# Two transformer layers: second chunk's token load, MLP weight loads and a norm buffer moved in the ramp, with a new instruction order

## The chip, the cores and the metric

The kernel runs on one core of a Trainium2 chip. The metric is the device time of one execution in microseconds (us), lower is better. Five engines work side by side: TensorE (PE) multiplies, VectorE (DVE), ScalarE (ACT) and GpSimd (POOL) compute on tiles, and SyncE (SP) issues the transfers (DMAs), transposing ones among them. Each engine runs its instructions strictly in the order in which the program holds them, and waits on semaphores for the others.

## The reference

The input is 2048 tokens of 576 features. Two layers of the same form run one after the other, with the same weights in both:

```python
qkv = (x @ wqkv) ... # 32 heads of 18 features
scores = einsum("bhqd,bhkd->bhqk", q, k) * (Dh ** -0.5)
mask = (idx[:, None] - idx[None, :] >= 0) & (idx[:, None] - idx[None, :] < 256)
p = softmax(where(mask, scores, -1e9))
o = einsum("bhqk,bhkd->bhqd", p, v)
A_ref = o ... @ wo
h = gelu(einsum("bsd,df->bsf", layernorm(x), w1) + b1)   # 576 -> 4608
B_ref = einsum("bsf,fd->bsd", h, w2) + b2                # 4608 -> 576
x = x + A_ref(layernorm(x));  x = x + B_ref(layernorm(x))   # twice
```

## The kernel before

**Tiles and chunks.** The tokens are cut into 16 tiles of 128, four tiles to a chunk, so that each layer has four chunks and the program eight (`k` from 0 to 7). A chunk goes through these steps: layer norm of its four tiles (`ln1_in` for the input tokens), with each normalised tile transposed into a buffer; projections to queries, keys and values (`qkv`); attention (`E0` for the first chunk, `E` for the others) in eight groups of four heads with up to three score pieces and one value product each; the output projection with residual, second norm and its transpose (`tail`); and the MLP, in three parts of a first matmul with gelu (`G_part`) and a second matmul (`mm2`). The attention of one chunk is interleaved with the MLP of the chunk before. Neither the ramp (first chunk's norm, projections, attention) nor the end has a partner of that kind.

**Buffers.** `xnTa` holds the transposed norm that the projections read, `xnTm[:, 0]` and `xnTm[:, 1]` the transposed norm that the MLP reads, for even and odd chunks. `x_in` is the upper half of the residual tensor `x_res`, seen as bf16; the input tokens are loaded there. `w1_sb` has three slots for blocks of the first MLP matrix, each filled by one large transfer and two small ones (`w1_load`). In traces the names are those of the tensors: a load of tokens shows as `x_res<-in_A_x_dram`, one of either MLP matrix as `w_sb<-in_B_w_dram`.

**Order.** Nothing is written out by hand. Every operation is handed to a planner (`Plan.add`) with the names that it reads and writes, an estimated cost and latency, and a priority. The planner then walks through time (`schedule`): of all operations whose predecessors are done it takes the one that can start earliest on its engine, and among equal starts the one with the lower priority number. The result is a fixed order on every engine; semaphore waits follow from the names. A table `PL.nudge` adds an offset of up to 300 in either direction to the priority of every named stage (`q0.v2` is the value projection of the first chunk's third tile, `ea3.1` a score group, `ld0` the loads of the ramp, and so on), which outweighs the priorities in the code. Where the planner foresees an idle PE in the first 140 us, it puts in matmuls on a zero tile (`warm_fn`, line 674) that compute nothing.

**The ramp's loads.** SP first issues the tokens of the first four tiles and the three weight matrices for queries, keys and values. What follows hangs on gates, names of results that a load reads only so as to be issued behind them:

- the tokens of tiles 4 to 7 (second chunk) read `xa3`, the last transposed norm tile of the first chunk;
- the tokens of tiles 8 to 11 (third chunk) and both bias loads read `k3`, the first chunk's last transposed key tile;
- of the first three blocks of the MLP's first matrix, the first reads `v0h0` (a value cast), the second reads `qx0`, a name that nothing has written at that point, so that it has no gate at all, and the third reads `aq2` (an attention group).

The norm of the first chunk is transposed on PE, as are its key tiles; the norm tiles of the second and third chunk and the query tiles are transposed by DMAs that SP issues (line 741 for norms, line 880 for queries and keys).

Lines that the prediction names: 626 is every plain transfer, 687 and 691 the norm's statistics, 700 and 702 its reciprocal root on POOL, 797 the projections of the first chunk, 778 and 781 those of the second chunk and all of the MLP's second matmul (one wide matmul, or four narrow ones side by side), 837 the projections of later chunks, 909 the scores, 919 the exponential, 940 the mask, 957 the value product, 1093 the MLP's first matmul.

Of the kernel before, what the change touches and what calls it, by code (L numbers as in the profile page):

```python
# [435 lines left out]
def build_kernel(nc, A_x, A_wqkv, A_wo, B_x, B_w1, B_b1, B_w2, B_b2, out):  # L436
    D = 576
# [41 lines left out]
    PL.nudge = {"": -86.31, "b": 23.63, "ea0.0": -264.23, "ea0.1": 170.66, "ea0.2": 170.75, "ea0.p0": -91.12, "ea0.p1": 0.1, "ea0.p2":  # L479
# [187 lines left out]
    for i in OUT:  # L667
        b = Bank((i,))
        add("pe", lambda e, b=b: zero(e, b), reads=["warm"], writes=[b], cost=0.25, lat=0.2, prio=-7, alloc=[b])
# [665 lines left out]
```

## Time and profile before

| | us |
|---|---|
| median of 3 runs | 863.51 |
| lowest, highest | 863.23, 866.3 |
| the profiled execution | 864.07 |
| its span in the trace | 862.3 |

| engine | busy us | share of the span |
|---|---|---|
| PE, matmuls | 846.4 | 98% |
| PE, weight loads | 520.0 | 60% |
| ACT | 601.2 | 70% |
| DVE | 395.7 | 46% |
| POOL | 378.6 | 44% |

The span runs from the first instruction to the last; the 1.8 us between it and the execution's own time lie around it. Matmuls are pipelined, so a busy PE is not a PE at its peak. In the views, "L741" is line 741 of the kernel; a row of the timeline gives start, duration, engine, line, operation, what it writes and reads, how many instructions were merged and, in brackets, the idle time before them with what ended it. "SPq" is the queue from which SP issues transfers. A granted clock of 1.00 is TensorE's full speed.

### The profile page before, as it was taken

The page shows a single profiled execution, that of the slowest core. Times are in us where ns is not written, and L with a number is a line of the kernel's source. Part 1 is how long each engine was busy: PE and PEld are TensorE (multiplying, and loading weights), DVE is VectorE, ACT ScalarE, POOL GpSimd, SP SyncE. Part 2 cuts the span into 40 slices and gives each one's busy share as a digit, 9 for nine tenths or more (in the row PEclk, how much of TensorE's full clock was granted, in tenths as well). Part 3 has the DMA queues.
Part 4 walks back from the last instruction along what each step waited for, and adds up shares of the span by engine and source line. Part 5 has one row for each costly group of instructions (what it writes and reads, how often), then busy time and mean ns, then how long its engine had stood idle before and what let it go on. Part 6 is the DMA issues. An engine that isn't in the chain of part 4 may idle for free.

```text
span 862.3 us, 27890 instructions
## 1 busy us (share of the span) xinstructions
PE 846.4 (98%) x12002; PEld 520.0 (60%) x12002; DVE 395.7 (46%) x949; ACT 601.2 (70%) x757; POOL 378.6 (44%) x563
## 2 busy tenths in 40 slices
PE   8899999999999999999999999999999999999998
PEld 6455556556565565666665655656556555556556
DVE  5787334644356442673426723465223633153012
ACT  5798797688757797476774878738777589853730
POOL 3787454375234662254522655416444276331100
PEclk9999999999999999999999999999999999999999
DMA  9798534743577524985359353594434963446320
GB/s 235 143 187 142 140 96 136 165 126 66 167 161 150 140 72 138 176 142 170 102 124 192 85 164 124 99 204 108 154 122 104 250 190 105 135 133 179 120 84 29
DMA packets 181995, 119.84 MB, mean 139 GB/s; under 512 B 107504, under 2 KB 181872, under 8 KB 181872
## 3 DMA queue, kind: packets, MB, share of 16 engines
q1 hardware_dynamic: 181872, 118.05, 55.6%
q8 instruction: 95, 1.56, 0.8%
q14 instruction: 28, 0.23, 0.1%
HBM read 90.10 MB, written 2.36 MB: 107 GB/s over the span
## 4 chain that ended last, share of the span: by engine, by line
PE 88%; DMA 4%; DVE 2%; POOL 2%; ACT 2%; issue 1%; SPq 0%; POOLq 0%; ACTq 0%
PE ps L1093 30%; PE ps L778 25%; PE ps L781 10%; PE ps L837 8%; PE ps L909 6%; PE ps L957 4%; PE ps L1048 3%; DMA xnTm<-xn 2%; ACT pT L919 1%; DMA xnTa<-xn 1%; PE ps L797 1%; POOL pT L940 1%; DVE xn L718 1%; DVE x_res L1025 1%; DMA qT<-qn 1%
## 5 line engine op out<-in xcount | busy, mean ns | idle before, releaser
L940 POOL TENSOR_SCALAR_AFFINE_SELECT pT<-pT 128x512 bf16<-128x512 bf16 (+1 forms) x368 | 284.3, 794 | 234.7 <-ACT pT L919 228.9
L919 ACT ACTIVATE pT<-ps 128x1024 bf16<-128x1024 f32 (+1 forms) x384 | 345.5, 972 | 49.9 <-PE ps L909 49.2
L1093 PE MATMUL ps<-xnTm,w_sb 64*128 64x512 bf16 x2592 | 290.9, 376 | 1.1 <-DVE vA L849 0.7
L1103 ACT ACTIVATE hT<-ps,b1col 128x512 bf16<-128x512 f32 x276 | 168.1, 688 | 175.3 <-PE ps L1093 175.0
L1093 PEld LDWEIGHTS ps<-xnTm,w_sb 64*128 64x128 bf16 x2592 | 129.6, 94 | 140.4 <-issue 4.8
L778 PE MATMUL ps<-w_sb,hT 128*128 128x288 bf16 x1446 | 193.7, 287 | 1.5 <-DVE x_res L1025 0.7
L1025 DVE TENSOR_TENSOR x_res<-ps,x_res 128x288 f32<-128x288 f32 x224 | 100.3, 453 | 183.5 <-PE ps L778 128.9
L778 PEld LDWEIGHTS ps<-w_sb,hT 128*128 128x128 bf16 x1446 | 133.6, 98 | 52.6 <-issue 17.1
L837 PE MATMUL ps<-wqkv,xnTa 64*128 64x288 bf16 x1296 | 90.8, 283 | 1.8 <-DMA xnTa<-xn 0.6
L781 PE MATMUL ps<-w_sb,hT 128*32 128x288 bf16 x2664 | 91.6, 286 | 0.2
L861 DVE CAST qn<-ps 128x288 bf16<-128x288 f32 x112 | 45.7, 448 | 99.1 <-PE ps L837 88.9
L837 PEld LDWEIGHTS ps<-wqkv,xnTa 64*128 64x128 bf16 x1296 | 61.6, 94 | 28.8 <-issue 3.1
L781 PEld LDWEIGHTS ps<-w_sb,hT 128*32 128x32 bf16 x2664 | 68.4, 97 | 14.9 <-issue 4.6
L968 DVE STREAM_TRANSPOSE oq<-ps 128x512 f32<-128x512 f32 x64 | 45.7, 714 | 66.6 <-PE ps L957 65.5
L909 PE MATMUL ps<-qT,kT 32*128 32x384 bf16 (+2 forms) x1216 | 64.2, 277 | 2.8 <-ACT pT L919 1.6
L700 POOL TENSOR_SCALAR vtmp<-mv_all 128x1 f32<-128x1 f32 (+1 forms) x43 | 8.9, 207 | 111.8 <-DVE mv_all L691 108.3
L687 DVE BATCH_NORM_STATS2 st_all<-x_res 128x6 f32<-128x288 f32 (+1 forms) x128 | 53.5, 445 | 9.0 <-DMA x_res<-in_A_x_dram 8.2
L1109 POOL TENSOR_TENSOR x_res<-x_res,b2bc 128x576 f32<-128x576 f32 x32 | 40.2, 1277 | 39.1 <-ACT hT L1103 38.9
L849 DVE CAST vA<-ps 128x288 bf16<-128x288 f32 x60 | 25.0, 447 | 56.6 <-PE ps L837 55.6
L957 PE MATMUL ps<-pT,vA 128*20 128x384 bf16 (+2 forms) x1408 | 50.4, 275 | 0.0
L909 PEld LDWEIGHTS ps<-qT,kT 32*128 32x128 bf16 x1216 | 19.4, 92 | 42.7 <-issue 29.8
L718 DVE TENSOR_SCALAR xn<-x_res,mv_all,rstd 128x576 bf16<-128x576 f32 (+1 forms) x60 | 34.4, 578 | 21.1 <-DMA xnTm<-xn 9.0
(58 smaller groups left out, 486.8 us busy)
## 6 DMA issues: line engine op xcount, KB each, us to landing
w_sb<-in_B_w_dram SPq DMA_DIRECT2D x46, 864.0 KB, 6.1
w_sb<-in_B_w_dram SPq DMA_DIRECT2D x48, 768.0 KB, 4.8
w_sb<-in_B_w_dram SPq DMA_DIRECT2D x96, 48.0 KB, 4.5
wqkv<-in_A_wqkv_dram SPq DMA_DIRECT2D x3, 576.0 KB, 4.8
x_res<-in_A_x_dram SPq DMA_DIRECT2D x3, 576.0 KB, 4.9
wqkv<-in_B_w_dram SPq DMA_DIRECT2D x2, 864.0 KB, 6.7
out_dram<-x_res SPq DMA_DIRECT2D x12, 144.0 KB, 1.8
wo_sb<-in_A_wo_dram SPq DMA_DIRECT2D x4, 144.0 KB, 3.0
```

The source lines that it names most:

```text
L687: add("dve", lambda e, i=i, s=s: e.bn_stats(st_all[:, t, i, :], s[:, t, i * HB:(i + 1) * HB]), reads=res, writes=[f"st{t}_{i}"], cost=0.37 ...
L778: return e.matmul(bank(b)[:, 0:HB], lhs, rhs, start=start, stop=stop, skip_group_check=True)
L781: ins = e.matmul(bank(b)[32 * j:32 * j + 32, 0:HB], lhs[:, 32 * j:32 * j + 32], rhs, start=start, stop=stop, tile_position=(0, 32 * j), sk ...
L837: ins = e.matmul(bank(bs[o])[:, 0:HB], xnTa[r:r + 64, c, i * 128:(i + 1) * 128], wqkv[r:r + 64, c, col:col + HB], start=(c == 4), stop=(ph ...
L861: add("dve", lambda e, b=bs[o], dst=dst: e.tensor_copy(dst, heads_of(bank(b))), reads=[bs[o]], writes=[f"qn{sl}h{o}"], cost=0.375, lat=0.1 ...
L909: ins = e.matmul(two(bs[j // 2])[:, j % 2, col:col + nq * 128], k_of(T0 + so)[0][32 * j:32 * j + 32, g, :], qs[32 * j:32 * j + 32, g, qo * ...
L919: add("act", lambda e, h2=h2: e.activation(pT[:, sl, 2 * h2:2 * h2 + 2, lo:hi], two(bs[h2])[:, :, lo:hi], ACT.Exp, scale=SCALE), reads=[bs ...
L940: add("pool", lambda e, ap=ap, pat=pat, sgn=sgn, kind=kind: e.affine_select(ap, ap, pattern=pat, compare_op=(ALU.is_ge if kind == "d" else ...
L957: ins = e.matmul(bank(bo)[32 * j:32 * j + VW, qo * 128:(qo + nq) * 128], vA[:, (T0 + so) % VS, 8 * j + g, :], pT[:, sl, j, col:col + nq * ...
L1025: add("dve", lambda e: e.tensor_tensor(x_res[:, t, sl], bank(b)[:, 0:HB], x_old[:, t, sl], ALU.add), reads=[b] + ([f"xin{t}"] if first els ...
L1093: ins = e.matmul(bank(bks[i])[:, 0:n], w1_sb[r:r + 64, sls[i], col:col + 128], xnTm[r:r + 64, k % 2, c, 0:n], start=(c == 4), stop=(ph == ...
L1103: add("act", lambda e, ff=ff, hd=hd, bk=bk: e.activation(hd[:, 0:n], bank(bk)[:, 0:n], ACT.Gelu_apprx_tanh, bias=b1col[:, ff:ff + 1]), rea ...
```

## The change

Five edits and a new table:

1. The tokens of the second chunk lose their gate and get priority -9.9, right behind the loads of the value weights (-10).
2. The second chunk's norm is transposed into `xnTm[:, 0]` (named `xm0_`) instead of `xnTa`, and its projections read it there. The first chunk's `tail` writes the same half later.
3. Of the MLP's first matrix, the first block is issued behind `xm0_3`, now the last norm tile of the second chunk, and the second block behind `k3`. The third keeps `aq2`.
4. The tokens of the third chunk are issued behind `xm0_3` instead of `k3`.
5. In `ln1_in`, which serves the second and the third chunk, reciprocal roots are made for two tiles at a time instead of four.

Beside these, some costs by which the planner reckons are altered, the second part of the first chunk's PE transposes names both of its inputs, and all of `PL.nudge` is replaced, so that the order on every engine is another one from the start to the end.

```diff
-    PL.nudge = {"": -86.31, "b": 23.63, "ea0.0": -264.23, ...
+    PL.nudge = {"": -1.63, "b": -20.47, "ea0.0": 108.12, ...
...
     def xin_load(a, cnt, reads=(), prio=-10):
...
-            cost=0.6, prio=prio)
+            cost=0.45 if a < 4 else 0.6, lat=1.4 if a < 4 else 2.0, prio=prio)
...
     def w_load(n, reads=()):
...
-            writes=[f"w{w}A"], cost=0.6, prio=-10)
+            writes=[f"w{w}A"], cost=0.5, lat=1.9, prio=-10)
...
-        add("pe", lambda e, b=b: zero(e, b), reads=["warm"], writes=[b], cost=0.25, lat=0.2, prio=-7, alloc=[b])
+        add("pe", lambda e, b=b: zero(e, b), reads=["warm"], writes=[b], cost=0.42, lat=0.2, prio=-7, alloc=[b])
...
-                add("pe", fn, reads=rd[cs[0] // 4:][:1] + ["ident"], writes=[b], cost=0.1 * len(cs), ...
+                add("pe", fn, reads=rd[:1 + cs[0] // 4] + ["ident"], writes=[b], cost=0.1 * len(cs), ...
...
-            wr = [f"w{w}A", f"xa{i}"] + [f"w{w}{x}{b}" for x in "BC" for b in range(2)]
+            xT, xn_ = (xnTm[:, 0], "xm0_") if k == 1 else (xnTa, "xa")
+            wr = [f"w{w}A", f"{xn_}{i}"] + [f"w{w}{x}{b}" for x in "BC" for b in range(2)]
             if k < KF:
-                bs = two_out(lambda c: xnTa[:, c, i * 128:(i + 1) * 128], ...
+                bs = two_out(lambda c: xT[:, c, i * 128:(i + 1) * 128], ...
...
-    xin_load(4, 4, ["xa3"], -6)
+    xin_load(4, 4, ["wvA"] if False else [], -9.9)
...
-    xin_load(8, 4, ["k3"], -4)
...
-        ln_rstd(list(range(t0, t0 + nt)), False, prio)
+            if t % 2:
+                ln_rstd([t - 1, t], False, prio)
         for i in range(nt):
-            ln_norm_T(t0 + i, i, xnTa, "xa", prio, x_in, [f"xin{t0 + i}"], dup=True)
+            ln_norm_T(t0 + i, i, *((xnTm[:, 0], "xm0_") if k == 1 else (xnTa, "xa")), prio, x_in, [f"xin{t0 + i}"], dup=True)
...
     ln1_in(1, -0.9)
+    xin_load(8, 4, ["xm0_3"], -0.8)
...
                 wo_load()
-                w1_load(-1, ["v0h0"])
+                w1_load(-0.7, ["xm0_3"])
...
             if k == 0:
-                w1_load(-1, ["qx0"])
+                w1_load(-1, ["k3"])
                 w1_load(-1, ["aq2"])
```

More of the change, by code (lines that the diff above doesn't have):

```diff
@@ L478, in build_kernel @@
     PL.turn = {"hc": 0.3, "rh": 0.05, "rc": 0.05, "ch": 0.3}
-    PL.nudge = {"": -86.31, "b": 23.63, "ea0.0": -264.23, "ea0.1": 170.66, "ea0.2": 170.75, "ea0.p0": -91.12, "ea0.p1": 0.1, "ea0.p2":
[64 rows of a table removed]
+    PL.nudge = {"": -1.63, "b": -20.47, "ea0.0": 108.12, "ea0.1": -112.05, "ea0.p0": -0.32, "ea0.p1": -13.77, "ea0.p2": -108.16,
[63 rows of a table added]
     def sb(name, shape, dtype):
@@ L736, in fn @@
                     return ins
-                add("pe", fn, reads=rd[cs[0] // 4:][:1] + ["ident"], writes=[b], cost=0.1 * len(cs), prio=prio, alloc=[b] if cs[0] == 0 else ())
+                add("pe", fn, reads=rd[:1 + cs[0] // 4] + ["ident"], writes=[b], cost=0.1 * len(cs), prio=prio, alloc=[b] if cs[0] == 0 else ())
             add("act", lambda e: e.copy(dst[:, :, i * 128:(i + 1) * 128], bank(b).bitcast(BF16)[:, 0:KD * 128].rearrange("p (c q) -> p c q", c=KD)),
@@ L823, in qkv @@
             dest = [f"v{A % VS}h{o}" for o in range(2)] if w == "v" else [f"qn{qn_ctr[0] % NQN}h{o}" for o in range(2)]
-            wr = [f"w{w}A", f"xa{i}"] + [f"w{w}{x}{b}" for x in "BC" for b in range(2)]
+            xT, xn_ = (xnTm[:, 0], "xm0_") if k == 1 else (xnTa, "xa")
+            wr = [f"w{w}A", f"{xn_}{i}"] + [f"w{w}{x}{b}" for x in "BC" for b in range(2)]
             if k < KF:
-                bs = two_out(lambda c: xnTa[:, c, i * 128:(i + 1) * 128], lambda c, s, n=n: wqkv[:, c, n * D + s:n * D + s + HB],
+                bs = two_out(lambda c: xT[:, c, i * 128:(i + 1) * 128], lambda c, s, n=n: wqkv[:, c, n * D + s:n * D + s + HB],
                              wr, prio + 0.01 * n, after=dest, fill=(6, 7) if k == 1 else FILL, mode="c" if k == 1 else "f")
```

127 rows, old and new, of the table add are left out of this document.

## The prediction

> **What bounds the kernel now.** I read the page first, for the engine that ends the span.
>
> ```profile
> PE 846.4 (98%) x12002; PEld 520.0 (60%) x12002; DVE 395.7 (46%) x949; ACT 601.2 (70%) x757; POOL 378.6 (44%) x563
> ```
>
> TensorE (PE) is busy for 98% of the span. A change of order and of load times removes no matrix work, so it can win only what PE does not use. Busy time by stage shows where that is. The two stages here are the ramp, from the first projection to the first MLP matmul, and what follows up to the last 22 us.
>
> ```profile
> 7.64:89.62 81.98, 74.21 (x1051) 45.70 (x1051) 58.78 (x150) 68.68 (x100) 52.64 (x89) 0.98 0.90 169
> 89.62:840.00 750.38, 746.69 (x10763) 454.63 (x10764) 325.64 (x770) 530.27 (x655) 320.95 (x458) 1.00 0.54 138
> ```
>
> The first column after the stage is its length, then PE busy, weight loads, DVE, ACT, POOL; near the end of the row stands the granted clock. The ramp leaves PE 81.98 - 74.21 = 7.77 us idle, more than twice the 750.38 - 746.69 = 3.69 us of the nine times longer stage behind it. What lies ahead of the ramp are the first loads with warm-up matmuls, which the change leaves as they are. So the ramp is the place, and the PE timeline and two narrow stages name its losses:
>
> ```profile
> 18.05 0.78 PE L797 MATMUL ps<-wqkv,xnTa 128*128 128x288 bf16 x5
> 20.06 0.34 PE L909 MATMUL ps<-qT,kT 32*128 32x384 bf16 x4 [1.23 <-DMA qT<-qn]
> ...
> 32.37 0.80 PE L781 MATMUL ps<-wqkv,xnTa 128*32 128x288 bf16 x20 [2.60 <-DMA xnTa<-xn]
> ```
>
> ```profile
> 29.77:32.37 2.60, 0.00 (x0) 0.00 (x0) 1.46 (x5) 1.56 (x3) 2.35 (x5) 1.00 1.10 81
> 33.97:37.35 3.38, 3.38 (x17) 1.69 (x17) 1.54 (x5) 3.02 (x4) 2.33 (x4) 0.50 0.35 70
> ```
>
> Three losses stand close together. PE waits 1.23 us for a transposed query tile before the first scores, and 2.60 us for the first transposed tile of the second chunk's norm. Then, from 33.97 to 37.35, the granted clock is 0.50 with PE busy throughout: 3.38 x 0.5 = 1.69 us lost.
>
> **What the losses hang on.** Both waits come out of the DMA queue of SyncE. Its timeline:
>
> ```profile
> 7.59 1.78 SPq L626 DMA_DIRECT2D w_sb<-in_B_w_dram  x3
> 9.56 4.12 SPq L880 DMA_TRANSPOSE qT<-qn  x2
> 13.73 0.59 SPq L626 DMA_DIRECT2D x_res<-in_A_x_dram  x1
> 14.93 1.58 SPq L880 DMA_TRANSPOSE qT<-qn  x1
> 19.29 0.37 SPq L626 DMA_DIRECT2D x_res<-in_A_x_dram  x1
> ...
> 22.57 1.24 SPq L880 DMA_TRANSPOSE qT<-qn  x1
> 24.52 1.57 SPq L626 DMA_DIRECT2D w_sb<-in_B_w_dram  x3
> 26.85 7.06 SPq L741 DMA_TRANSPOSE xnTa<-xn  x4
> ```
>
> And the issues of some of these moments, with KB of each and us to landing: the MLP weights of 7.59, the tokens of 13.73, the query tiles of 14.93 and of 22.57, then the norm tiles issued before 29.5 and after it.
>
> ```profile
> w_sb<-in_B_w_dram SPq DMA_DIRECT2D x1, 768.0 KB, 6.0
> x_res<-in_A_x_dram SPq DMA_DIRECT2D x1, 576.0 KB, 5.2
> qT<-qn SPq DMA_TRANSPOSE x1, 5.0
> qT<-qn SPq DMA_TRANSPOSE x1, 3.0
> xnTa<-xn SPq DMA_TRANSPOSE x2, 5.1
> xnTa<-xn SPq DMA_TRANSPOSE x3, 2.6
> ```
>
> The same transpose lands in 3.0 us with nothing large ahead, and in 5.0 us behind the 576 KB of tokens; a norm tile in 2.6, and in 5.1 behind the 768 KB of weights. The tokens themselves were issued at 13.73 only because they wait for the first chunk's last norm tile, and DVE's first statistics of that chunk wait for them:
>
> ```profile
> 19.00 1.18 DVE L687 BATCH_NORM_STATS2 st_all<-x_res 128x6 f32<-128x288 bf16 x3 [2.41 <-DMA x_res<-in_A_x_dram]
> ```
>
> **The change, part by part.** *Tokens of the second chunk behind the value weights.* They take the place that the MLP weights have at 7.59. Those landed 6.0 us later, at 13.6, with 768 KB; 576 KB should need no longer, so 13.6 is the late bound, against 19.00 now: 5.4 us sooner. From first statistics to first landed norm tile the chain now takes 32.37 - 19.00 = 13.4 us. At that length the tile is there at 27.0 or before. PE has other work until 29.77, or 28.5 when the first wait is gone, so the 2.60 us go whole, with 1.5 us to spare. I take 2.60, bounds 0 and 2.60.
>
> *First scores.* With no tokens at 13.73, the query tile of 14.93 lands after 3.0 rather than 5.0 us, at 17.9. PE's projection work ends at 18.05 + 0.78 = 18.83, so the wait of 1.23 goes. Were the landing still 5.0, nothing would; I take 1.23, the row of 22.57 being the same operation with a free queue.
>
> *Clock.* The half clock begins 1.60 us after the gap of 2.60. The ramp's mean clock of 0.98 leaves room for no second such stretch (0.02 x 81.98 = 1.64), so the gap of 1.23 has none behind it. I take the 1.69 us as gone with the gap; bounds 0 and 1.69. [...]
>
> *MLP weights later.* The block of 7.59 now waits for the key tile that released the tokens of 19.29, the block of 24.52 for the second chunk's last norm tile. They are read from the first MLP matmul on, at 89.62, some 60 us later: no cost by themselves. In the queue, the three transfers of 7.59 now start at about 19.3 or later; if they stand ahead of the norm tiles, those land in 5.1 rather than 2.6 us, 2.5 later: 29.5 against 28.5, and 1 us of the wait is back. That case is priced below.
>
> *Tokens of the third chunk* wait for the same norm tile, about 27 instead of 19.29. SyncE's queue holds what follows until then: the second chunk's query and key transposes, which need that norm anyway, and, if the order puts it there, the first chunk's fourth query tile, now at 22.57. The consumer is far:
>
> ```profile
> 53.40 1.21 SPq L741 DMA_TRANSPOSE xnTa<-xn  x1
> ...
> 80.40 1.20 SPq L741 DMA_TRANSPOSE xnTm<-xn  x1
> ```
>
> ```profile
> L778 PE MATMUL ps<-wqkv,xnTa x90: 283/286/447, 33.9 to 59.7; 128*128 128x288 bf16 x90
> ```
>
> The third chunk's norm goes out at 53.40, over 20 us after the new landing. Cost nothing.
>
> *Norm in a buffer of its own.* The second chunk no longer waits for the first chunk's projections to leave xnTa. In exchange the first chunk's post-attention norm, which writes that half of xnTm at 80.40, waits for the second chunk's last projection, now at 59.7: 20 us of slack, no cost. The third chunk's norm may start earlier than 53.40, since xnTa is free; I count nothing for it.
>
> *Reciprocal roots in pairs.* For each of two chunks one pair of POOL operations more:
>
> ```profile
> 23.63 1.02 POOL L702 TENSOR_TENSOR rstd<-vtmp,nhalf 128x4 f32<-128x4 f32 x1
> ```
>
> The longer of the two took 1.02 us for four tiles, which bounds what it adds for each chunk, and POOL is busy for only 52.64 of the ramp's 81.98 us; the first two tiles need not wait for the other two. Cost nothing; without that cover some of it would stand on the norm chain, inside its 1.5 us of slack. The second transpose's extra wait is for an input of the copy it already waits for. The planner's new costs act through the order alone.
>
> *Order found anew.* Every priority is replaced, so each engine's order changes over the whole span. To the good, the stage from 89.62 to 840 has 3.69 us idle. To the bad, short attention runs cut the MLP's:
>
> ```profile
> 102.37 3.85 PE L781 MATMUL ps<-w_sb,hT 128*32 128x288 bf16 x120
> 106.16 0.34 PE L909 MATMUL ps<-x_res,xnTm 32*128 32x384 bf16 x4
> ...
> 113.06 0.91 PE L781 MATMUL ps<-w_sb,hT 128*32 128x288 bf16 x24
> 113.90 0.40 PE L909 MATMUL ps<-x_res,kT 32*128 32x256 bf16 x8
> ```
>
> From start to next start, 120 matmuls took 3.79 us, 0.76 for each 24; a run of 24 alone took 0.84. A cut costs 0.08 us. If all 64 value products (8 chunks by 8 groups) came to stand alone, 5.1 us. Between -3.7 and +5.1 I take 0: both orders fill the same work into the same engines.
>
> **The sum.** 2.60 + 1.23 + 1.69 = 5.52 us. It carries to the end, as PE is the bound behind 89.62. ACT could refuse it, since the exponentials fill most of the ramp. Its own waits leave room:
>
> ```profile
> 33.98 1.51 ACT L919 ACTIVATE pT<-ps 128x768 bf16<-128x768 f32 x2 [2.65 <-PE ps L909]
> 35.72 1.51 ACT L919 ACTIVATE pT<-ps 128x768 bf16<-128x768 f32 x2 [0.22 <-PE ps L909]
> 38.16 7.22 ACT L919 ACTIVATE pT<-ps 128x768 bf16<-128x768 f32 x10 [0.93 <-PE ps L909]
> ```
>
> These are 3.80 us, with the earlier start of 1.23 it makes 5.03: nearly the same. The profiled execution took 864.07 us, so 858.55; it lay 0.56 above the median of 863.51, so I forecast 858.0.
>
> **Rivals.** *The slow clock stays* (0.13). If gaps as short as these do not halve the clock, or another short gap does, 1.69 stays: 859.7. For it speaks the delay of 1.60 us; against it, that it comes once, right after the ramp's longest gap. [...]
>
> *The wait comes back* (0.18). The moved weight block gets ahead of the norm tiles, and DVE, busy with casts, is late with the statistics; PE idles at about 29 as now. 2.60 and 1.69 stay, only 1.23 goes: 862.3. It decides when the chain is over 1.5 us later than reckoned. The landings of 5.1 and 2.6 speak for it, the 5.4 us of earlier tokens against.
>
> *New waits behind the ramp* (0.15; slower). The new order leaves PE with nothing to run while an MLP's norm tiles land: 2.6 us, the shortest landing, at a chunk's start. Four such starts (10.4) outweigh 5.5 and the half percent; at five, 13.0 - 5.5 = 7.5 more: 871.0. Against it: in the order of now, under nearly the same dependences, such a start costs no more than this, the longest wait of that stage:
>
> ```profile
> PE ps L1093 <- DVE vA L849: 0.7, 1, 0.7
> ```
>
> *More than the three waits* (0.12). Of the ramp's loss, 7.77 idle + 1.69 clock, 3.94 us remain beyond the sum; the free xnTa lets the third chunk's projections fill them. With three quarters, 855.0.
>
> **How the numbers follow.** The forecast keeps 0.42; its own range is 854.3 to 863.1 by the order's bounds. About half a percent, 4.3 us, is what a measurement of this kernel can tell from no change: 859.2 and 867.8. Under 859.2 lie two thirds of the forecast (0.28), a third of the first rival (0.04), a tenth of the second (0.02) and nearly all of the last (0.11): 0.45. Above 867.8 lie 0.12 of the slower rival and 0.03 of bad orders elsewhere: 0.15. The rest is 0.40. For 8 in 10, 852 to 867.
>
> **What would show it.** Right: tokens issued at about 7.6; first statistics before 14; first scores by 19; no PE wait over 1 us on a norm tile; granted clock 1.00 through the ramp; first MLP matmul at about 84. Wrong: PE idle beyond 3.69 us in the 750 us behind it, a new clock drop, or a first MLP matmul as late as 89.

## The result

The changed kernel takes 858.65 us (median of 6 runs, 857.42 to 858.81), the kernel before took 865.0 us in 6 runs beside it (863.23 to 866.9). The ratio is 0.9922 with a 95% interval of 0.9905 to 0.9939: faster, by 0.8%. The forecast was 858.0 us. The profiled execution took 858.81 us with a span of 857.1 us, 5.2 us less than the 862.3 us of before.

The stages of the changed kernel, in the columns of the prediction's table: the loads, the ramp, the long stage behind it, the end. The last row is a narrow piece at the start of the ramp.

```profile
PE 843.6 (98%) x11968; PEld 514.4 (60%) x11968; DVE 399.1 (47%) x949; ACT 600.2 (70%) x757; POOL 380.0 (44%) x567
...
0.00:8.55 8.55, 4.71 (x27) 3.13 (x28) 5.50 (x17) 2.46 (x4) 5.32 (x18) 0.96 0.77 236
8.55:86.14 77.59, 73.04 (x1057) 45.63 (x1058) 56.28 (x145) 65.58 (x97) 51.86 (x90) 0.98 0.91 178
86.14:834.90 748.76, 746.53 (x10732) 450.42 (x10729) 330.93 (x774) 532.20 (x656) 322.83 (x460) 1.00 0.54 138
...
7.90:11.10 3.20, 2.55 (x12) 1.70 (x13) 1.20 (x4) 0.00 (x0) 0.47 (x3) 0.50 0.98 298
```

The first MLP matmul now starts at 86.14 instead of 89.62, so 3.48 us of the 5.2 are won up to there. The other 1.72 us are won behind it, 1.46 of them as idle time of the long stage, which went from 3.69 to 748.76 - 746.53 = 2.23 us. PE's idle time in the ramp fell from 7.77 to 77.59 - 73.04 = 4.55 us. But the ramp starts later, at 8.55 instead of 7.64, and its granted clock is still 0.98.

PE's timeline shows both:

```profile
8.55 2.56 PE L796 MATMUL ps<-wqkv,xnTa 128*128 128x288 bf16 x10 [2.15 <-DMA wqkv<-in_A_wqkv_dram]
...
20.75 0.34 PE L909 MATMUL ps<-qT,kT 32*128 32x384 bf16 x4
...
30.34 1.41 PE L780 MATMUL ps<-wqkv,xnTm 128*32 128x288 bf16 x40
```

Neither of the two waits of before has a bracket any more: the first scores and the first projection of the second chunk start right behind other work. What is new is the wait of 2.15 us at the start, for query weights, and the half clock that goes with it: the ten matmuls behind it take 2.56 us, where ten at full clock take 1.39 to 1.45 (at 11.29 and 12.85).

SyncE's queue and the two moments that it sets, DVE's first statistics of the second chunk and, further down, ACT's first exponential:

```profile
8.53 0.59 SPq L625 DMA_DIRECT2D x_res<-in_A_x_dram  x1
11.64 7.14 SPq L880 DMA_TRANSPOSE qT<-qn  x3
19.34 3.85 SPq L740 DMA_TRANSPOSE xnTm<-xn  x3
23.25 1.30 SPq L880 DMA_TRANSPOSE qT<-qn  x1
24.64 1.25 SPq L740 DMA_TRANSPOSE xnTm<-xn  x1
27.34 0.39 SPq L625 DMA_DIRECT2D x_res<-in_A_x_dram  x1
27.79 1.74 SPq L625 DMA_DIRECT2D w_sb<-in_B_w_dram  x3
```

```profile
14.72 1.17 DVE L686 BATCH_NORM_STATS2 st_all<-x_res 128x6 f32<-128x288 bf16 x3
```

```profile
19.80 2.07 ACT L878 COPY kT<-ps 128x1024 bf16<-128x1024 bf16 x2
21.77 0.82 ACT L919 ACTIVATE pT<-ps 128x768 bf16<-128x768 f32 x1
```

The tokens go out at 8.53, the statistics start at 14.72 (19.00 before), the first norm tile goes out at 19.34 with nothing large ahead of it, and both weight blocks follow behind the last norm tile.

### The profile page after: what moved, and what is told of

It is laid out like the page before. It is cut to its first block, busy times and chain, and to the rows that moved or that the text cites. A ratio compares the mean times of both kernels' runs of the same rounds, so it can differ in the third digit from the quotient of the medians.

```text
span 857.1 us, 27818 instructions
## 1 busy us (share of the span) xinstructions
PE 843.6 (98%) x11968; PEld 514.4 (60%) x11968; DVE 399.1 (47%) x949; ACT 600.2 (70%) x757; POOL 380.0 (44%) x567
## 4 chain that ended last, share of the span: by engine, by line
PE 92%; DMA 2%; ACT 2%; DVE 2%; issue 1%; POOL 1%; SPq 0%; ACTq 0%; DVEq 0%; POOLq 0%
PE ps L1093 32%; PE ps L777 25%; PE ps L780 10%; PE ps L837 8%; PE ps L909 6%; PE ps L957 5%; PE ps L1048 4%; PE ps L796 1%; ACT pT L919 1%; DMA xnTa<-xn 1%; DMA wqkv<-in_A_wqkv_dram 1%; DMA xnTm<-qn 1%; DVE oq L968 1%; DMA kT<-qn 0%; DVE x_res L1025 0%
## 5 line engine op out<-in xcount | busy, mean ns | idle before, releaser
L1093 PEld LDWEIGHTS ps<-xnTm,w_sb 64*128 64x128 bf16 x2592 | 126.4, 94 | 141.3 <-issue 4.3
L699 POOL TENSOR_SCALAR vtmp<-mv_all 128x1 f32<-128x1 f32 (+2 forms) x45 | 9.2, 204 | 123.4 <-DVE mv_all L690 122.1
L1048 PE MATMUL ps<-wo_sb,attT 64*128 64x288 bf16 x576 | 43.2, 283 | 0.3
```

The costliest lines, as they stand in the source:

```text
L1048: ins = e.matmul(bank(bs[o])[:, 0:HB], attT[r:r + 64, c, i * 128:(i + 1) * 128], wo_sb[r:r + 64, c, col:col + HB], start=(ph == 0 and c == ...
L1093: ins = e.matmul(bank(bks[i])[:, 0:n], w1_sb[r:r + 64, sls[i], col:col + 128], xnTm[r:r + 64, k % 2, c, 0:n], start=(c == 4), stop=(ph == ...
```

## The experiments

Swapping a priority lets the planner find a new order everywhere. So, apart from the two kernels with exchanged tables at the end, the finished order of one kernel was kept, and only what is named was moved; all other engines keep their sequence. Ratios are to the kernel before on the same chip. That kernel was run 57 times with them, with chip medians of 865.4, 865.4 and 865.28 us.

### What the loads do in the old order

First, in the kernel before, SyncE alone was reordered:

```diff
 SP: value weights of the first chunk
+SP: tokens 4-7                      (were behind xa3)
-SP: MLP block 1 (768 KB and two small ones)
...
-SP: MLP block 2
 SP: norm tiles of the second chunk x4
+SP: MLP blocks 1 and 2
 SP: transposes of the second chunk's queries
```

> The old program with its order kept on every engine but SyncE: the second chunk's tokens are issued right behind the value weights without a gate, and the first two blocks of the MLP weights behind the second chunk's four norm tiles. Theory (the ramp's waits were the cost, the queue made them): the wait of 1.23 us before the first scores goes; the wait of 2.60 for the norm tile shrinks to about 1, because VectorE's order still puts that norm behind the value casts at 25.9; the half clock of 3.4 us goes with it: 3 to 4.5 us less, about 861. Rival (the gain came from the new order, not from the loads): less than 1 us.

Measured: 869.0 us, ratio 1.004 (1.0025 to 1.0055), slower by 3.6 us. Both waits of before are gone, yet a longer one stands later in the ramp. First the norm tiles of the second chunk, the landing of the first of them, and the projection that waited for it:

```profile
25.84 7.06 SPq L741 DMA_TRANSPOSE xnTa<-xn  x4
```

```profile
xnTa<-xn SPq DMA_TRANSPOSE x1, 2.6
```

```profile
28.69 0.80 PE L781 MATMUL ps<-wqkv,xnTa 128*32 128x288 bf16 x20
```

DVE keeps its old order here, and both chunks share `xnTa`; still the wait of 2.60 us is gone. The first tile is issued only 1.0 us sooner than before (26.85), but it lands after 2.6 us, where that of before, with a weight block ahead of it, took 5.5. From the first projection to the matmul at 39.44 PE takes 31.76 us; for the same work the kernel before takes 35.96 us (7.64 to 43.60). The clock is 1.00 up to there. So the loads alone, in the old order, win 4.2 of the forecast 5.52 us by that point.

What follows loses more than that. SyncE's queue and its longest wait, PE, and the clock of a stretch around it (the number third from the end):

```profile
32.96 4.32 SPq L626 DMA_DIRECT2D w_sb<-in_B_w_dram  x6
42.02 1.25 SPq L880 DMA_TRANSPOSE x_res<-qn  x1
```

```profile
SPq L132 <- DMA w_sb<-in_B_w_dram: 4.6, 1, 4.6
```

```profile
45.84 1.38 PE L778 MATMUL ps<-wqkv,xnTa 128*128 128x288 bf16 x5 [5.61 <-DVE qn L861]
```

```profile
44.80:51.70 6.90, 5.86 (x60) 2.93 (x60) 3.33 (x8) 2.78 (x4) 1.23 (x2) 0.51 0.64 145
```

With six weight transfers in one place, SyncE is held for 4.6 us until a landing of `w_sb`, and the query transpose behind it goes out only at 42.02. What it is that holds SyncE there, the trace does not say. DVE's next cast into `qn` has to wait until that transpose has read it, and PE waits for the cast:

```profile
45.32 0.46 DVE L861 CAST qn<-ps 128x288 bf16<-128x288 f32 x1 [6.17 <-DMA x_res<-qn]
```

Where the weights are put is thus a part of the change in its own right.

The same once more, with the two blocks at different places:

```diff
+SP: tokens 4-7 behind the value weights
-SP: MLP block 1 behind the value weights
...
 SP: transpose of the first chunk's fourth query tile
+SP: MLP block 1
-SP: MLP block 2
 SP: norm tiles of the second chunk x4
+SP: MLP block 2
```

> As the run with the tokens first in the old program, but with the two weight blocks apart: one behind the fourth query tile, one behind the four norm tiles, so that SyncE isn't held before the second chunk's query tiles. Theory (the queue made the waits; the 5.6 us of the earlier run came from two blocks in one place): no wait over 1.5 us on a norm tile and none for query tiles, clock 1.00 from 34 on, first MLP matmul at 85 to 87, 3 to 4.5 us less than before: 861 to 862.5. Rival (without a new order the loads bring nothing): 864.5 or more.

Measured: 863.11 us, ratio 0.9979 (0.9967 to 0.9991), 2.2 us below the kernel before. The new stall is gone, and of the old ones one. Its queue, the landing of the first norm tile, DVE's first statistics of the second chunk, and PE:

```profile
8.31 0.59 SPq L626 DMA_DIRECT2D x_res<-in_A_x_dram  x1
...
22.99 1.95 SPq L626 DMA_DIRECT2D w_sb<-in_B_w_dram  x3
26.56 5.74 SPq L741 DMA_TRANSPOSE xnTa<-xn  x3
```

```profile
xnTa<-xn SPq DMA_TRANSPOSE x1, 5.3
```

```profile
17.45 1.17 DVE L687 BATCH_NORM_STATS2 st_all<-x_res 128x6 f32<-128x288 bf16 x3
```

```profile
8.38 1.39 PE L797 MATMUL ps<-wqkv,xnTa 128*128 128x288 bf16 x10 [2.07 <-DMA wqkv<-in_A_wqkv_dram]
...
19.70 0.34 PE L909 MATMUL ps<-qT,kT 32*128 32x384 bf16 x4
...
31.90 0.80 PE L781 MATMUL ps<-wqkv,xnTa 128*32 128x288 bf16 x20 [2.42 <-DMA xnTa<-xn]
```

The tokens are issued at 8.31, nearly as in the changed kernel, and the wait ahead of the first scores is gone. But a weight block stands ahead of the norm tiles, the first of which lands 5.3 us after its issue, and PE still waits 2.42 us. DVE is not the cause. The statistics run at 17.45, in the place that the old order gives them, and in the run before this one they do so too, at 16.74, without a wait. Counted from the first projection, both kernels issue the first norm tile at the same moment (26.56 - 8.38 = 18.18 us and 25.84 - 7.68 = 18.16 us). They differ in its landing, 5.3 against 2.6 us, and that is the wait: the case that the prediction priced with 5.1 against 2.6.

No run moved the weights and left the tokens late. An estimate from the rows of the kernel before: its first norm tile, issued at 26.85, would have been there at 29.45 with a landing of 2.6 us, and PE was ready at 29.77, or at 28.5 with the first wait gone. How much of the 2.60 us the early tokens win in the old order, beside the weights, therefore stays open.

### Where the weights stand in the new order

```diff
 SP: value weights
+SP: MLP block 1
 SP: tokens 4-7
...
-SP: MLP block 1                     (behind the norm tiles)
```

> The changed program, order kept, with the first MLP weight block of 864 KB ahead of the second chunk's tokens again. Theory (the tokens must come first): they land about 2.5 us later, at 16.5, VectorE waits 1.8 us for them at 14.7 with the query casts queued behind, and the first scores come 1.5 to 2 us later: 860 to 860.7. Rival (there is slack): no change from 858.65 within 0.4.

Measured: 860.65 us, 2.0 us above the changed kernel; ratio 0.9942 (0.9927 to 0.9958). DVE now waits for tokens:

```profile
15.76 1.18 DVE L686 BATCH_NORM_STATS2 st_all<-x_res 128x6 f32<-128x288 bf16 x3 [1.95 <-DMA x_res<-in_A_x_dram]
```

The second chunk's projections still start without a wait; its norm is 1 us later and uses up slack. Of the 1.8 us that the span grows, 0.4 lie ahead of the first MLP matmul and 1.4 behind it; no run explains the latter. So the order in which block and tokens are issued is worth 2.0 us, for the most part not by way of the wait of 2.60.

### The norm's own buffer

In the changed kernel the second chunk's norm was put back into `xnTa`. A norm tile then waits for the first chunk's value projection of the same tile, so each was moved behind it on SyncE; in the first kernel the loads keep their place, in the second they go behind all four tiles.

```diff
-xT, xn_ = (xnTm[:, 0], "xm0_") if k == 1 else (xnTa, "xa")
+xT, xn_ = (xnTa, "xa")
...
+e9 only: SP: tokens 8-11, biases and MLP blocks behind the last norm tile
```

> The changed program, order kept on all engines but SyncE, with the second chunk's norm back in the buffer that the first chunk's projections read, so that each norm tile is issued only behind the value projection that reads the old one. Theory (the own buffer is needed for the wait to go): TensorE waits 1 to 3 us for the first norm tile at about 30, more for the later ones, and the clock may halve after it: 860.5 to 864. Rival (the buffer matters little, the early tokens do it): within 0.5 us of 858.65.

> As the run with the shared norm buffer in the changed program, but with all four norm tiles ahead of the third chunk's tokens and of both weight blocks, so that only the buffer differs. Theory (the own buffer is needed in this order): TensorE still waits 1.5 to 3 us for the first norm tile at about 30, and the clock may halve: 860.5 to 863. Rival (the 9 us of the earlier run were the weights ahead of the tiles): within 0.7 us of 858.65.

Measured: 867.77 us (ratio 1.0021, 1.0008 to 1.0034) with the loads in between, 863.77 us (0.9981, 0.9966 to 0.9996) with the norm tiles first: 9.1 and 5.1 us above the changed kernel. PE of the first, then queue and PE of the second:

```profile
36.78 2.59 PE L780 MATMUL ps<-wqkv,xnTa 128*32 128x288 bf16 x40 [7.46 <-DMA xnTa<-xn]
```

```profile
25.95 7.16 SPq L740 DMA_TRANSPOSE xnTa<-xn  x4
```

```profile
8.94 2.56 PE L796 MATMUL ps<-wqkv,xnTa 128*128 128x288 bf16 x10 [2.44 <-DMA wqkv<-in_A_wqkv_dram]
...
33.90 1.41 PE L780 MATMUL ps<-wqkv,xnTa 128*32 128x288 bf16 x40 [3.10 <-DMA xnTa<-xn]
```

With one buffer the norm tiles go out from 25.95 to 31.7 instead of 19.34 to 24.64, although tokens and statistics (15.11) are within 0.4 us of the changed kernel's, and a wait is back, of 3.10 us. It is not for the first tile, which lands after 2.6 us, at 28.55, before PE is ready for it at 30.80. What lands just ahead of 33.90 is the third, issued at 29.9 and there 3.9 us later. In the new order the own buffer takes this wait away; in the old order, as the first kernel of the study showed, there was none with a shared buffer. In the first of these two kernels the wait is 4.4 us longer, and the clock is at half from 32.8 to 39.6, 6.83 us where the stretch of before lasts 3.41; the loads between its norm tiles are the only difference.

### The clock

In the kernel before, 20 matmuls on the zero tile were put into the gap of 2.60 us, so that PE has no gap there but starts no sooner:

```diff
 PE: scores of the first chunk
+PE: 20 matmuls on the zero tile
 PE: first projection of the second chunk
```

> The old program with 20 matmuls on the zero tile put before the matmul that waits 2.60 us for the norm tile, so that TensorE is busy in the gap and the wait itself stays. Theory (the half clock follows the gap): the granted clock stays 1.00 from 34 to 37 and 1.7 us go, about 863.3 against 865.0. Rival one (the clock drop has another cause): it stays, no change. Rival two (the exponentials on ScalarE set the pace there): the clock is full and the time is the same within 0.5 us.

Measured: 862.69 us, ratio 0.997 (0.9958 to 0.9982), 2.7 us below the kernel before, though the second chunk's projections start later than before, at 34.23:

```profile
31.81 2.36 PE L674 MATMUL ps<-warm 128*128 128x256 bf16 x20
34.23 0.80 PE L781 MATMUL ps<-wqkv,xnTa 128*32 128x288 bf16 x20
```

The filled gap has no half clock behind it, and the mean clock is 1.00. Of the 12 runs of this kernel 9 have a mean clock of 1.000, of the 57 of the kernel before 11. So the clock term of the sum is real. Its size is read from the medians, not from this profile, in which the first MLP matmul starts at 89.56, as before (89.62): the ramp began 0.8 us later here, and the second chunk's projections 1.9 us later. The runs of the kernel before show its size without any edit. Sorted by the mean clock granted, their medians are:

| mean clock | runs | median us |
|---|---|---|
| 1.000 | 11 | 863.12 |
| 0.998 | 32 | 865.28 |
| 0.996 | 14 | 867.36 |

A step of 0.002 over 863 us is 1.7 us, one stretch of 3.4 us at half clock; each step costs 2.1 to 2.2 us. (Runs that differ in the clock may differ in the gap ahead of the stretch too; this table does not part the two.) The profile of before was taken at 0.998, with one stretch.

In the changed kernel the stretch has moved to the start. There the gap was filled in the same way:

```diff
 PE: transposes of the first chunk's norm
+PE: 10 matmuls on the zero tile
 PE: first projection of the first chunk
```

> The changed program with 10 more matmuls on the zero tile before its first projection, which waited 2.15 us for the query weights and then ran at half clock from 7.9 to 11.3. Theory (the half clock follows the gap and its 1.7 us count at the start of the ramp): clock 1.00 throughout, 1 to 1.7 us less than 858.65, about 857.3. Rival (ScalarE's exponentials, without pause from 21.8 on, set the pace): the same within 0.4 us.

Measured: 859.05 us, ratio 0.9929 (0.9907 to 0.9951): no gain in the median. The six runs fall into two groups, three from 857.28 to 857.62 and three from 860.48 to 861.98, for which no run gives a reason. The profiled one is of the faster group, and in it the start is as early as could be wished:

```profile
7.87 1.39 PE L796 MATMUL ps<-wqkv,xnTa 128*128 128x288 bf16 x10 [0.31 <-ACT xn L722]
...
19.70 0.34 PE L909 MATMUL ps<-qT,kT 32*128 32x384 bf16 x4
```

The first MLP matmul starts at 85.92, only 0.22 us before that of the changed kernel, while the first scores start 1.05 us before. The runs of the changed kernel say the same: three with a mean clock of 0.998 have a median of 858.68, three with 1.000 of 858.53. Between the first scores and the MLP something else sets the pace.

### What sets the pace of the rest of the ramp

The candidate was ACT, whose exponentials start at 21.77, right behind two key copies. Two key copies and two casts were moved to DVE, in the second kernel with the filled start as well:

```diff
-ACT: key copies 3 and 4, query and key casts of the fourth tile
+DVE: the same, at the same place in the order
...
+e11 only: PE: 10 matmuls on the zero tile ahead of the first projection
```

> The changed program with two key copies (1.0 us each) and two query and key casts (0.4 us each) of the first chunk moved from ScalarE to VectorE, order kept. Theory (in the changed program the exponentials on ScalarE set the ramp's pace from 21.8 to 61): 1.5 to 2.5 us less, 856.2 to 857.2. Rival (something else sets the end of the ramp, such as TensorE or GpSimd's masks): within 0.5 us of 858.65.

> The run before it with 10 more matmuls on the zero tile ahead of the first projection, so that the clock doesn't halve at the start. Theory: with ScalarE relieved the start of the ramp counts, another 0.5 to 1.5 us less: 855 to 856.5. Rival: the same as without the filling within 0.4 us.

Measured: 857.4 us (857.19 to 857.79; ratio 0.9908, 0.9893 to 0.9922) and 857.66 us (856.33 to 858.36; 0.9906, 0.989 to 0.9922). ACT of the first of the two:

```profile
18.76 1.01 ACT L878 COPY kT<-ps 128x1024 bf16<-128x1024 bf16 x1
20.11 1.51 ACT L919 ACTIVATE pT<-ps 128x768 bf16<-128x768 f32 x2 [0.34 <-PE ps L909]
```

The exponentials start 1.66 us sooner than in the changed kernel, and the median is the lowest of all, 1.25 us below the changed kernel. Its interval and that of the changed kernel overlap, though, and three of the six runs with the filled start alone are below 857.7 too. In the first kernel's profile the query weights also landed sooner (first projection at 7.44, 8.55 in the changed kernel), and the filled start brought nothing on top of the moved copies. So it is not settled that ACT sets the pace, and neither kernel is clear of the changed one, with medians 1.0 and 1.25 us below it.

### The two tables of priorities

> The changed program with the old table of priorities. Theory (waits): the loads alone bring most of it, 859 to 861. Rival (the new order brings it): 864 or more, since the table was not found for this program.

> The old program with the new table of priorities. Theory (waits): the norm tile's wait stays, 864 or more. Rival (the new order brings it): 860 or less.

```diff
-PL.nudge = {its own table}
+PL.nudge = {the other kernel's table}
```

Measured: the new code with the old table takes 944.09 us (ratio 1.0915, 1.0893 to 1.0937), the old code with the new table 930.87 us (1.0757, 1.0734 to 1.078). The three longest waits of PE in the first (times, and the longest):

```profile
PE ps L1094 <- DMA xnTm<-xn: 18.2, 2, 12.1
PE ps L910 <- ACT pT L920: 16.9, 26, 2.0
PE ps L838 <- DMA xnTa<-xn: 11.7, 2, 7.1
```

PE's idle time lies all over the span. Neither table fits the program for which it was not found, so these two runs don't divide the gain into code and order. They do show what a badly fitting order costs: some 65 to 80 us.

## Why the prediction was right, and where only its sum was

**The bound and the place: right.** PE stays at 98% busy, and the ramp gave most of the gain.

**The wait of 2.60 us: gone as forecast, by the mechanism that it gave.** The signs came: tokens at 8.53 (forecast about 7.6), no wait at the second chunk's first projection at 30.34. First statistics at 14.72 missed "before 14": the tokens left 0.9 us later than reckoned, and a cast of DVE stood ahead when they had landed. In the old order the loads alone were enough (no wait at 28.69), and a weight block left ahead of the norm tiles brought 2.42 us back, as the rival of the returning wait had it. The margin was smaller there than the 1.5 us that were reckoned: the first tile landed at 25.84 + 2.6 = 28.44, 0.25 us before PE was ready, because the statistics came at 16.74 and not at 13.6. In that order the first tile is issued only 1.0 us sooner, and its landing takes 2.9 us less; the 5.4 us of earlier tokens show in the new order alone.

What the step had at no cost and no gain is the buffer of its own. In the new order DVE makes the norm earlier (its first normalised tile at 18.55, at 25.93 before), and there a shared `xnTa` holds the tiles back and leaves a wait of 3.10 us: a tile that is ready sooner runs into the first chunk's projections, which still read the buffer.

**The wait of 1.23 us: gone, but not turned into time in this profile.** The query tiles issued at 15 to 19 us land after 3.2 us (forecast 3.0). The first scores start at 20.75 rather than "by 19", 0.69 us later than before, since the ramp starts 0.91 us later and at half clock. In the first kernel of the study, whose ramp starts at 7.68, they do start at 19.00.

**The clock term of 1.69 us: real, slightly small, and it did not vanish.** Filling the gap alone gave 2.7 us, and one stretch costs 2.1 to 2.2 us by the runs of before. The forecast of 1.00 throughout the ramp failed: the stretch stands at the start now. It seems to cost less there: the three runs at 0.998 and the three at 1.000 differ by 0.15 us in their medians, though only one of them was profiled. Compared at equal mean clock, the change is worth 863.12 - 858.53 = 4.6 us at 1.000 and 865.28 - 858.68 = 6.6 us at 0.998; the difference of 2.0 would be what a stretch costs in the old place and not in the new one (the runs are from several chips, on which the kernel before differs by 0.4 us at most). So the rival of the slow clock was half right: the stretch stays, but at a place where it costs little.

No run shows why a gap has a half clock behind it in one run and none in the next. The stretches themselves last 3.41 us in the profiles of before, the change and the kernel with norm tiles first, and 6.83 us around each of the gaps of 5.61 and 7.46. Length and PE's busy time of the 3.41 us just ahead of the stretch, in before, in the change and in the kernel with norm tiles first (there also of two pieces around the gap of 3.10 us):

```profile
30.52:33.93 3.41, 1.56 (x45) 1.03 (x46) 1.39 (x5) 0.81 (x2) 2.21 (x5) 1.00 0.89 68
```

```profile
4.41:7.82 3.41, 1.34 (x13) 0.69 (x10) 2.64 (x9) 1.18 (x3) 1.90 (x5) 1.00 1.03 343
```

```profile
4.81:8.22 3.41, 1.13 (x11) 0.49 (x8) 2.95 (x9) 1.18 (x3) 1.72 (x5) 1.00 1.02 322
...
28.70:32.11 3.41, 2.10 (x24) 1.12 (x22) 1.48 (x4) 3.39 (x6) 2.33 (x3) 1.00 0.60 90
32.11:35.52 3.41, 1.57 (x45) 1.11 (x49) 0.61 (x2) 0.26 (x1) 1.23 (x2) 1.00 0.58 102
```

Ahead of a stretch PE is idle for 1.85, 2.07 and 2.28 us of the 3.41. Around the gap of 3.10 us it is idle for 1.31 and 1.84 us of the two pieces, 3.15 together, the clock stays at 1.00 in both, and no stretch follows. So 1.84 us of 3.41 stand without a stretch and 1.85 with one, and neither the length of a gap nor the idle time around it tells in these profiles which gap is followed by a half clock, and the 1.60 us between gap and half clock in the kernel before are not explained either.

**The order, taken as 0 between -3.7 and +5.1: mis-sized by -1.7.** Span less start of the first MLP matmul is 771.9 to 772.9 us in the four profiles with the old order (before and three experiments) and 770.0 to 772.3 in the seven with the new one (the change and six experiments), with means of 772.6 and 770.9. One of the seven, with the weight block first, lies among the old ones, so the size is an estimate from single profiles. The new waits of the slower rival did not come; the changed kernel's longest behind the ramp is this:

```profile
PE ps L837 <- DMA xnTa<-xn: 0.8, 1, 0.8
```

**The sum: right by compensation.** Forecast were 5.52 us in the ramp and 0 behind it; measured are 3.48 and 1.72 in the profiles. "First MLP matmul at about 84" was 86.14. Of the 2 us missing in the ramp the later start and its half clock explain little: with the start filled, the first scores came 1.05 us sooner and the first MLP matmul only 0.22 us. So they are lost in between. The prediction asked whether ACT could refuse the sum and put that at half a microsecond (5.03 against 5.52). With copies taken off ACT the first MLP matmul came at 84.42, with the filled start as well at 85.70; whether it was ACT stays open. The order gave nearly the same back. That the sum of 5.5 and the 5.2 of the spans agree is thus in part luck. The tie to a median of 863.51 was also off: the kernel before runs at 865.0 to 865.4 on longer measurement, with a mean clock below 1.000 in 46 of 57 runs, and two of the three first runs were on the low side.

## What to carry to other kernels

When a load is pulled forward, follow it to the engine that consumes it and to the buffer that its result goes into: here a weight block ahead of the norm tiles in the queue kept the wait alive in one order (2.42 us), and a shared buffer did so in the other (3.10 us). Look also at what is pushed away: two weight blocks issued together in a new place held the queue for 4.6 us and cost more than the loads had won. And judge a gain by more than the total: a stage table of before and after shows whether a sum came out by its own terms or by others.

## What the runs showed of the hardware beyond that

The landing of the query weights, which no edit touches, varies by a microsecond: in the profile of before the first projection started at 7.64 without waiting for them, in a kernel with the same start (the filled gap) it waited 1.97 us for them, to 8.43, and in the changed kernel to 8.55. The half clock starts while PE is still idle (0.50 from 7.90, the first matmul at 8.55), and around the two longer gaps, of 5.61 and 7.46 us, it lasts 6.83 us. In the first kernel of the study PE was idle for the first 1.00 us of that; in the stretches of 3.41 us, in before, the change and the kernel with norm tiles first, it was idle for at most 0.73 us. Half clock came with gaps of 2.15, 2.44 and 2.60 us and not with 2.07, 2.42 and 3.10, so in these profiles the length of a gap is no forecast. DVE copied a key tile in 0.68 us where ACT took 1.01:

```profile
20.09 0.68 DVE L1334 COPY kT<-ps 128x1024 bf16<-128x1024 bf16 x1
```
